# Keys loaded a second time in transposed layout, decayed by elementwise products, in place of matmul transposes

## The chip, the cores and the metric

The program runs on 1 core of one Trainium2 chip. The metric is the device time of one execution in microseconds (us), the median over several runs. The traces come from one profiled execution whose own time is given beside its span. Engines are named TensorE (PE; its weight loads PEld), VectorE (DVE), ScalarE (ACT), GpSimd (POOL) and SyncE (SP, which here only issues DMAs).

## The reference, cut to what matters

Three layers follow each other, all in fp32. Only the first is touched by the change. It is a linear recurrence over 768 steps for 4 batches x 8 heads, head dimension 48:

```
for t in range(768):
    cur    = u * k[t] outer v[t]
    y[t]   = r[t] @ (state + cur)
    state  = w[:, None] * state + k[t] outer v[t]
x = y as 3072 tokens x 384
logits = x @ phi                      # 32 slots, softmax over tokens and over slots
slot   = softmax_tokens(logits).T @ x
out_s  = relu(slot_e @ w1[e]) @ w2[e] # 8 experts, 4 slots each
x      = softmax_slots(logits) @ out_s
out    = gelu_sigmoid(x @ w_in) @ w_out   # w_in, w_out held as 64-bit floats
```

## The kernel before, in words

The recurrence is computed in chunks. A unit is one batch and one chunk of 128 steps; there are 24 units, taken two batches at a time, and each covers all 8 heads as 4 pairs. Powers of w stand in tables: `tr` holds the factor for every step of a chunk, in a layout with the head dimension on partitions (128 partitions x 4 pairs x 128 steps), and `tab` the reversed factor with steps on partitions. With r multiplied by `tr` and k by the reversed factor, a chunk is a masked product of r and k, then a product with v, plus a product of r with the carried state.

One pass of the loop over n (line 657) writes the instructions of several units into the in-order queues of the engines, in an order set by hand (`tc.manual_schedule`, line 361). For pass n they are: `r_decay(n+2)`, line 495, VectorE, r times `tr`, both in SBUF; `st_a(n+1)`, line 514, 16 matmuls of k and r into PSUM, whose halves are then masked, one by VectorE (line 518) and one by a ScalarE copy and a GpSimd select (lines 521, 522); `st_q`, line 531, matmuls on `rk`, copied to `qT` by ScalarE (line 534); `st_n(n-1)`, line 549, transposes of the output, with VectorE's add into `xn` (line 553); `bonus(n)`, line 538, a GpSimd product of v and a broadcast factor; `k_turn(n+2)`, lines 500 to 505: four TensorE transposes of the decayed key `kp` into the PSUM tile `k_ps`, a ScalarE copy of it to `kT`, and VectorE's product `rk` of r and `k_ps`; `st_y`, `st_u`, `st_v` (lines 603, 576, 614); `st_s`, VectorE's update of the carried state (lines 591, 592) and its ScalarE copies (line 595); `st_x` (lines 558, 561); `k_decay(n+3)`, line 488, a GpSimd product of k and `tab` (VectorE for the first units). Every fourth pass runs the token softmax of a group of four units ahead of the transposes of the next (lines 169 to 237).

From pass 3 on, `wload` (line 635) adds to each pass three of the four VectorE operations that decode a slice of `w_in` from 64-bit floats (lines 94 to 107). Of these all but line 94 read two tensors in SBUF. `wload` also issues DMAs of `w_in` and of the expert weights: 18 of them, 768 KB each, for experts 0 to 3 and half of expert 4, paced by the pass. All DMAs are issued by SyncE in program order; r of unit n+5 (`ld_r`, 256 KB) and k and v of unit n+5 (`ld_kv`, 384 KB) in pass n. The buffers of four of the five k and v tiles lie in the place of the second weight of expert 4 (`stage`, line 310), so the DMAs of that weight come after the last pass.

After the loop follow the slot inputs, the experts (lines 865 to 896), whose weights are partly loaded only then, and the last layer with its 1152 matmuls at line 1178.

Of the kernel before, what the change touches and what calls it, by code (L numbers as in the profile page):

```python
# [8 lines left out]
F32 = mybir.dt.float32  # L9
# [6 lines left out]
ALU = mybir.AluOpType  # L16
# [5 lines left out]
def attn_moe_mlp_kernel(  # L22
    ctx: ExitStack,
    tc: tile.TileContext,
    rT: bass.AP,
    kvn: bass.AP,
    r: bass.AP,
    w: bass.AP,
# [8 lines left out]
    nc = tc.nc  # L37
# [3 lines left out]
    E, _, FE = w1.shape  # L41
# [258 lines left out]
    with ExitStack() as actx:  # L300
# [4 lines left out]
        def at(shape, name, dt=F32, bufs=1):  # L305
            return ap.tile(shape, dt, tag=name, name=name, bufs=bufs)

        NRT, NKV, NKP, NXN, NXT, NA = 5, 5, 3, 6, 4, 2

        stage = wts.tile([P, FT * DM], F32, tag=f"wb{NSL}", name="stage")  # L310
        used = [0]

        def part(shape):

# [18 lines left out]
        qT = at([P, P], "qT")  # L333
        rt = [at([P, NP, P], f"rt{i}") for i in range(NRT)]
        kp = [at([P, H, HP], f"kp{i}") for i in range(NKP)]
        kT = at([P, NP, P], "kT")
        rk = at([P, NP, P], "rk")
        am = [at([P, 2, NP, P], f"am{i}") for i in range(NA)]
        sbd = [at([P, NP, 2, HP], f"sbd{i}") for i in range(2)]
# [11 lines left out]
        def ld_r(i):  # L351
            if 0 <= i < NU:
                b, c = units[i]
                nc.sync.dma_start(out=rt[i % NRT].rearrange("p q t -> p (q t)"), in_=rT[b, c])

        def ld_kv(i):
            if 0 <= i < NU:
                b, c = units[i]
                nc.sync.dma_start(out=kv[i % NKV], in_=kvn[b, c * P:(c + 1) * P])

        with tc.manual_schedule():
            wc = at([P, NP], "wc")
            uc = at([P, NP], "uc")
            nc.sync.dma_start(out=wc, in_=w)
            ld_kv(0)
            ld_r(0)
            nc.sync.dma_start(out=uc, in_=u)
            for i in range(1, NRT):
                ld_kv(i)
                ld_r(i)  # L370
                if i == 2:
                    nc.sync.dma_start(out=phn, in_=phi.rearrange("(k p) s -> p k s", p=P))
            make_identity(nc, ident)
# [73 lines left out]
            def small_tables():  # L447
                tt(out=w128.unsqueeze(2), in0=pb[:, :, 16:17], in1=pb[:, :, 16:17], op=ALU.mult)

                for m in range(2):  # L450
                    tt(
                        out=ubd[HP * m:HP * m + HP, :, m:m + 1], in0=uc[HP * m:HP * m + HP].unsqueeze(2),
                        in1=pa_[HP * m:HP * m + HP, :, 1:2], op=ALU.mult,
                    )
# [31 lines left out]
            def k_decay(i, eng=nc.gpsimd):  # L486
                if ok(i):
                    eng.tensor_tensor(
                        out=kp[i % NKP][:, :, 0:D], in0=kv[i % NKV][:, 0], in1=tab, op=ALU.mult
                    )  # L490

            def r_decay(i):
                if ok(i):
                    x = rt[i % NRT]
                    tt(out=x, in0=x, in1=tr, op=ALU.mult)

            def k_turn(i):

                if ok(i):
                    for q in range(NP):  # L500
                        nc.tensor.transpose(  # L501
                            k_ps[:, q, :], kp[i % NKP][:, 2 * q:2 * q + 2, :].rearrange("p h d -> p (h d)"), ident
                        )
                    nc.scalar.copy(out=kT, in_=k_ps)  # L504
                    tt(out=rk, in0=rt[i % NRT], in1=k_ps, op=ALU.mult)  # L505

            def st_a(i):

                if ok(i):
                    t = [ps.tile([P, NP, P], F32, tag="a", name="pa", bufs=2) for _ in range(2)]  # L510
                    for q in range(NP):
                        for m in range(2):
                            p = slice(HP * m, HP * m + D)
                            nc.tensor.matmul(  # L514
                                t[m][:, q, :], kT[p, q, :], rt[i % NRT][p, q, :], start=True, stop=True
                            )
                    x = am[i % NA]
                    nc.vector.copy_predicated(
                        out=x[:, 0], mask=mask.unsqueeze(1).to_broadcast([P, NP, P]), data=t[0]
                    )  # L520
                    nc.scalar.copy(out=x[:, 1], in_=t[1])  # L521
                    nc.gpsimd.affine_select(  # L522
                        out=x[:, 1], in_=x[:, 1], pattern=[[0, NP], [1, P]], compare_op=ALU.is_gt, fill=0.0,
                        base=0, channel_multiplier=-1,
                    )
# [102 lines left out]
                return [xn[:, (4 * g + m) % NXN, :] for m in range(4)]  # L628


            eq = [(e, n) for e in range(NSL + 1) for n in range(4 if e < NSL else 2)]
            wq = [(g, n) for g in range(NWI) for n in range(4)]
            NEQ = len(eq)

# [18 lines left out]
            put_tab()  # L653
            fill(9)
            small_tables()
            k_decay(0, nc.vector)
            for n in range(-2, NU + 2):
                g, m = divmod(n - 5, 4)
                first, second = (0 <= g < NG and m == x for x in range(2))
                second = second and g < NG - 1  # L660
                r_decay(n + 2)
                if second:
                    grp.rows(g, (1,))
                st_a(n + 1)
                st_q(n + 1)
                if -1 <= n <= 0:
                    fill(8)
                if first:
                    g1(g)
                st_n(n - 1)  # L670
                if second:
                    grp.sums(g, g3_x(g), n=(0,))
                bonus(n)
                k_turn(n + 2)
                if n == -2:
                    fill(8)
                if first:
                    grp.maxima(g)
                if second:
                    grp.sums(g, None, n=(1,))  # L680
                st_y(n)
                st_u(n)
                st_v(n)
                st_s(n)
                st_x(n)
                if n == -1:
                    fill(7)
                if first and g < NG - 1:
                    grp.rows(g, (0,))
                k_decay(n + 3, nc.gpsimd if n > -1 else nc.vector)  # L690
                if n == 1:
                    flag()
                    flag_out()
                    selector()
                if n == 4:
                    n_ok = nc.values_load(flg, min_val=0, max_val=P * NP)
                if n >= 0:
                    ld_r(n + NRT)
                    ld_kv(n + NKV)
                wload(n)  # L700
                if n == NU - 1:
                    while eq:
                        load_w(*eq[0], wts, eq[0][0])
                        eq.pop(0)
                    for a in (2, 3):
                        load_w(NSL, a, wts, NSL)

            slot_inputs(
# [509 lines left out]
                    dec_two(n + 4)  # L1218


_INS = ["rT", "kv", "r", "w_l", "u_l", "moe_phi", "moe_w1", "moe_w2", "moe2_w_in", "moe2_w_out"]
_OUTS = [((3072, 384), "float32")]


# [39 lines left out]
```

## Time and profile before

| | |
|---|---|
| median of 3 runs | 437.15 us (436.16 to 437.56) |
| profiled execution | 435.27 us, span 433.8 us |
| TensorE, busy | 414.3 us (96%) |
| VectorE, busy | 263.3 us (61%) |
| ScalarE, busy | 189.5 us (44%) |
| GpSimd, busy | 61.2 us (14%) |
| DMA | 59.50 MB, mean 137 GB/s |
| granted TensorE clock, mean | 0.996 |

The shares are means over stages that differ. The recurrence lasts from about 10 to 155 us; the matmuls at line 1178 fill the second half of the span, where GpSimd does nothing and VectorE's share is below its mean. To read what a change of the recurrence is worth, one looks at the stretches of the recurrence, at the length of a pass, and at what each queue does in a pass.

### The profile page before, as it was taken

The page shows a single profiled execution, that of the slowest core. Times are in us where ns is not written, and L with a number is a line of the kernel's source. Part 1 is how long each engine was busy: PE and PEld are TensorE (multiplying, and loading weights), DVE is VectorE, ACT ScalarE, POOL GpSimd, SP SyncE. Part 2 cuts the span into 40 slices and gives each one's busy share as a digit, 9 for nine tenths or more (in the row PEclk, how much of TensorE's full clock was granted, in tenths as well). Part 3 has the DMA queues.
Part 4 walks back from the last instruction along what each step waited for, and adds up shares of the span by engine and source line. Part 5 has one row for each costly group of instructions (what it writes and reads, how often), then busy time and mean ns, then how long its engine had stood idle before and what let it go on. Part 6 is the DMA issues. An engine that isn't in the chain of part 4 may idle for free.

```text
span 433.8 us, 9269 instructions
## 1 busy us (share of the span) xinstructions
PE 414.3 (96%) x3746; PEld 362.3 (84%) x3746; DVE 263.3 (61%) x491; ACT 189.5 (44%) x450; POOL 61.2 (14%) x89
## 2 busy tenths in 40 slices
PE   8999999999999989987899999999999999999996
PEld 7877777777777755444799999999999999999996
DVE  5678788878788854235699974444454444544441
ACT  2455566564665633334668764222232222422221
POOL 4343443444334210000000000000000000000000
PEclk9999999999999999998999999999999999999999
DMA  7355987798868377994333003000030000300003
GB/s 250 142 173 184 284 304 240 243 322 256 286 204 288 101 278 251 382 382 156 80 121 111 0 2 109 2 0 2 0 110 0 2 0 2 109 2 0 2 0 109
DMA packets 36003, 59.50 MB, mean 137 GB/s; under 512 B 3057, under 2 KB 21617, under 8 KB 35953
## 3 DMA queue, kind: packets, MB, share of 16 engines
q1 hardware_dynamic: 35952, 58.85, 40.4%
q8 instruction: 30, 0.49, 0.5%
q14 instruction: 21, 0.16, 0.1%
HBM read 53.53 MB, written 4.72 MB: 134 GB/s over the span
## 4 chain that ended last, share of the span: by engine, by line
PE 53%; DMA 2%; DVE 2%; ACT 1%; SPq 1%; issue 1%; ACTq 0%; DVEq 0%
PE o L1178 45%; PE hpa L1116 3%; DMA raw_a<-in_moe_w_out_dram 2%; PE hpb L1116 2%; PE sop L893 1%; PE hp L869 1%; DVE glb L1130 1%; SPq L958 1%; PE htp L881 0%; PE ga L1088 0%; ACT ggb L1119 0%; DVE w_lo L988 0%; ACT G L1100 0%; DVE ghb L1129 0%; DVE raw_a L107 0%
## 5 line engine op out<-in xcount | busy, mean ns | idle before, releaser
L1178 PE MATMUL o<-w_hi,ghb 128*128 128x384 f32 x384 | 115.9, 335 | 0.0
L1178 PE MATMUL o<-w_lo,ghb 128*128 128x384 f32 x384 | 115.7, 334 | 0.0
L1178 PE MATMUL o<-w_hi,glb 128*128 128x384 f32 x384 | 115.5, 334 | 0.0
L1119 ACT ACTIVATE ggb<-hpa 128x512 f32<-128x512 f32 x64 | 38.2, 598 | 118.0 <-PE hpa L1116 117.9
L1129 DVE CAST ghb<-ggb 128x768 fp32r<-128x768 f32 x48 | 26.9, 560 | 83.9 <-ACT ggb L1119 83.9
L1178 PEld LDWEIGHTS o<-w_hi,ghb 128*128 128x128 f32 x384 | 70.2, 188 | 2.4
L1178 PEld LDWEIGHTS o<-w_hi,glb 128*128 128x128 f32 x384 | 71.1, 188 | 0.0
L1178 PEld LDWEIGHTS o<-w_lo,ghb 128*128 128x128 f32 x384 | 71.0, 188 | 0.0
L1130 DVE TENSOR_TENSOR glb<-ggb,ghb 128x768 fp32r<-128x768 f32 x64 | 61.3, 958 | 12.7 <-ACT ghb L1127 11.1
L505 DVE TENSOR_TENSOR rk<-rt,k_ps 128x512 f32<-128x512 f32 x24 | 16.5, 688 | 21.0 <-ACT kT L504 21.0
L1116 PE MATMUL hpa<-c4T,G 96*128 96x512 f32 x64 | 25.5, 398 | 2.7 <-ACT ggb L1119 1.3
L618 ACT COPY yT<-y_ps 128x512 f32<-128x512 f32 x24 | 14.0, 585 | 31.9 <-PE y_ps L614 31.8
L514 PE MATMUL pa<-rt,kT 48*128 48x128 f32 x384 | 27.9, 285 | 0.0
L514 PEld LDWEIGHTS pa<-rt,kT 48*128 48x128 f32 x384 | 23.3, 187 | 3.8 <-issue 3.3
L522 POOL TENSOR_SCALAR_AFFINE_SELECT am<-am 128x512 f32<-128x512 f32 x24 | 15.7, 655 | 73.5 <-ACT am L521 67.8
L1119 ACT ACTIVATE ggb<-hpb 128x256 f32<-128x256 f32 x64 | 24.2, 378 | 0.0
L504 ACT COPY kT<-k_ps 128x512 f32<-128x512 f32 x24 | 14.1, 586 | 21.8 <-PE k_ps L501 21.8
L603 PE MATMUL y_ps<-rt,sbd 128*128 128x128 f32 x160 | 21.2, 276 | 0.0
L614 PE MATMUL y_ps<-am,stage 128*48 128x128 f32 x320 | 21.1, 274 | 0.0
L603 PEld LDWEIGHTS y_ps<-rt,sbd 128*128 128x128 f32 x160 | 19.4, 192 | 0.6 <-issue 0.6
L501 PE MATMUL k_ps<-ident,kp 128*128 128x128 f32 x96 | 15.1, 280 | 4.8 <-ACT qT L534 3.7
L501 PEld LDWEIGHTS k_ps<-ident,kp 128*128 128x128 f32 x96 | 10.1, 140 | 11.0 <-issue 11.0
(185 smaller groups left out, 611.3 us busy)
## 6 DMA issues: line engine op xcount, KB each, us to landing
w<-in_moe_w_dram SPq DMA_DIRECT2D x32, 768.0 KB, 7.0
stage<-in_kv_dram SPq DMA_DIRECT2D x20, 384.0 KB, 3.8
rt<-in_rT_dram SPq DMA_DIRECT2D x24, 256.0 KB, 3.8
raw<-in_moe_w_in_dram SPq DMA_DIRECT2D x16, 384.0 KB, 4.3
out_dram<-obuf SPq DMA_DIRECT2D x24, 192.0 KB, 2.0
raw_a<-in_moe_w_out_dram SPq DMA_DIRECT2D x10, 384.0 KB, 3.6
raw_b<-in_moe_w_out_dram SPq DMA_DIRECT2D x6, 384.0 KB, 6.0
kv<-in_kv_dram SPq DMA_DIRECT2D x4, 384.0 KB, 3.8
```

Of the source, the lines that this page charges most:

```text
L501: nc.tensor.transpose(k_ps[:, q, :], kp[i % NKP][:, 2 * q:2 * q + 2, :].rearrange("p h d -> p (h d)"), ident)
L504: nc.scalar.copy(out=kT, in_=k_ps)
L505: tt(out=rk, in0=rt[i % NRT], in1=k_ps, op=ALU.mult)
L514: nc.tensor.matmul(t[m][:, q, :], kT[p, q, :], rt[i % NRT][p, q, :], start=True, stop=True)
L522: nc.gpsimd.affine_select(out=x[:, 1], in_=x[:, 1], pattern=[[0, NP], [1, P]], compare_op=ALU.is_gt, fill=0.0, base=0, channel_multiplier=-1,)
L603: nc.tensor.matmul(y_ps[:, q, :], sbd[b % 2][:, q].rearrange("p m d -> p (m d)"), rt[i % NRT][:, q, :], start=(q == 0), stop=False, skip_g ...
L614: nc.tensor.matmul(y_ps[HP * m:HP * m + D, q, :], kv[i % NKV][:, 1, 2 * q + m, :], am[i % NA][:, m, q, :], start=(c == 0 and q == 0), stop ...
L1116: nc.tensor.matmul(hp, G4[:, f * P:(f + 1) * P], c4T[:, c * TB + t0:c * TB + t0 + n], start=True, stop=True)
L1119: nc.scalar.activation(out=ggb[:, i % NB_S, t0:t0 + n], in_=hp, func=AF.Gelu_apprx_sigmoid)
L1129: nc.vector.tensor_copy(out=gh, in_=gg)
L1130: nc.vector.tensor_tensor(out=gl, in0=gg, in1=gh.bitcast(F32), op=ALU.subtract)
L1178: nc.tensor.matmul(o, x, y, start=f == 0 and i == 0, stop=f == KF - 1 and i == 2)
```

## The change

The host makes a second array of k, `kT`, padded and transposed as it does for r. SyncE loads it unit by unit (`ld_kt`, 256 KB each) into six tiles that lie in the place of the first weight of expert 4. `kt_decay` multiplies such a tile in place by `tr` read backwards: units 0 to 2 on VectorE, the others on GpSimd right behind `k_decay`. `k_turn` is gone; its product `rk` stays on VectorE and reads the new tile instead of PSUM, and `st_a` reads the new tile. Since the place of expert 4's first weight is now taken, both its halves are loaded after the last pass's other DMAs, and 16 loads instead of 18 are paced by the passes. `kp` and `k_decay` stay as they are.

```diff
+        stage_k = wts.tile([P, KD * FE], F32, tag=f"wa{NSL}", name="stage_k")
+        kt = [
+            stage_k[:, i * NP * P:(i + 1) * NP * P].rearrange("p (q t) -> p q t", q=NP) for i in range(NKT)
+        ]
...
+        def ld_kt(i):
+            if 0 <= i < NU:
+                b, c = units[i]
+                nc.sync.dma_start(out=kt[i % NKT].rearrange("p q t -> p (q t)"), in_=kTd[b, c])
...
+            ld_kt(0)
+            ld_r(0)
             ld_kv(0)
-            ld_r(0)
...
             for i in range(1, NRT):
+                ld_kt(i)
+                ld_r(i)
                 ld_kv(i)
-                ld_r(i)
...
-            def k_turn(i):
-
+            def kt_decay(i, eng=nc.gpsimd):
                 if ok(i):
-                    for q in range(NP):
-                        nc.tensor.transpose(
-                            k_ps[:, q, :], kp[i % NKP][:, 2 * q:2 * q + 2, :].rearrange("p h d -> p (h d)"), ident
-                        )
-                    nc.scalar.copy(out=kT, in_=k_ps)
-                    tt(out=rk, in0=rt[i % NRT], in1=k_ps, op=ALU.mult)
+                    x = kt[i % NKT]
+                    eng.tensor_tensor(out=x, in0=x, in1=tr[:, :, ::-1], op=ALU.mult)
+
+            def r_times_k(i):
+
+                if ok(i):
+                    tt(out=rk, in0=rt[i % NRT], in1=kt[i % NKT], op=ALU.mult)
...
-                                t[m][:, q, :], kT[p, q, :], rt[i % NRT][p, q, :], start=True, stop=True
+                                t[m][:, q, :], kt[i % NKT][p, q, :], rt[i % NRT][p, q, :], start=True, stop=True
...
-            eq = [(e, n) for e in range(NSL + 1) for n in range(4 if e < NSL else 2)]
+            eq = [(e, n) for e in range(NSL) for n in range(4)]
...
+            kt_decay(0, nc.vector)
+            r_decay(0)
             k_decay(0, nc.vector)
+            kt_decay(1, nc.vector)
             for n in range(-2, NU + 2):
...
-                r_decay(n + 2)
+                if n > -2:
+                    r_decay(n + 2)
...
-                k_turn(n + 2)
+                r_times_k(n + 2)
...
                 k_decay(n + 3, nc.gpsimd if n > -1 else nc.vector)
+                if n > -2:
+                    kt_decay(n + 3, nc.gpsimd if n > -1 else nc.vector)
...
                     ld_r(n + NRT)
+                    ld_kt(n + NRT)
                     ld_kv(n + NKV)
...
-                    for a in (2, 3):
+                    for a in range(4):
                         load_w(NSL, a, wts, NSL)
```

## Rows read from the trace of the kernel before

**Rows 1.** Busy time by stretch: from:to and length, engines busy (count), clock, DMA share, GB/s
```profile
35.46:140.57 105.11, 99.78 (x1382) 79.81 (x1381) 87.40 (x162) 61.65 (x165) 41.95 (x51) 1.00 0.81 265
140.57:155.70 15.13, 14.86 (x197) 11.84 (x197) 12.21 (x25) 8.30 (x26) 3.70 (x5) 1.00 0.44 150
...
165.60:199.60 34.00, 30.70 (x372) 15.42 (x364) 13.88 (x39) 13.52 (x27) 0.31 (x1) 0.99 0.94 339
```

**Rows 2.** Timeline of TensorE around the transposes: start, length, instruction, count, idle before
```profile
110.06 0.66 PE L549 MATMUL n_ps<-ident,yT 128*128 128x128 f32 x4
111.46 0.63 PE L501 MATMUL k_ps<-ident,kp 128*128 128x128 f32 x4 [0.74 <-ACT qT L534]
111.92 1.06 PE L603 MATMUL y_ps<-rt,sbd 128*128 128x128 f32 x8
```

**Rows 3.** Groups of VectorE, 35.46 to 140.57: count | busy us, mean ns | idle
```profile
L505 DVE TENSOR_TENSOR rk<-rt,k_ps 128x512 f32<-128x512 f32 x17 | 11.7, 688 | 14.2 <-ACT kT L504 14.2
L495 DVE TENSOR_TENSOR rt<-rt,tr 128x512 f32<-128x512 f32 x17 | 11.6, 683 | 0.0
L592 DVE TENSOR_TENSOR sc<-sc,w 128x192 f32<-128x192 f32 x13 | 9.5, 729 | 0.4
...
L107 DVE SCALAR_TENSOR_TENSOR win<-sq,win 128x384 f32<-128x384 f32 x13 | 8.0, 618 | 0.3
```

**Rows 4.** Timelines of GpSimd and VectorE around 78, 66, 121 and 107 us
```profile
78.08 1.01 POOL L488 TENSOR_TENSOR kp<-stage,tab 128x384 f32<-128x384 f32 x1
...
78.33 0.69 DVE L505 TENSOR_TENSOR rk<-rt,k_ps 128x512 f32<-128x512 f32 x1 [1.20 <-ACT kT L504]
...
66.09 1.14 POOL L488 TENSOR_TENSOR kp<-stage,tab 128x384 f32<-128x384 f32 x1 [1.44 <-issue]
...
66.29 1.35 DVE L107 SCALAR_TENSOR_TENSOR win<-sq,win 128x384 f32<-128x384 f32 x1
...
121.55 0.36 DVE L592 TENSOR_TENSOR sc<-sc,w 128x192 f32<-128x192 f32 x1
...
105.61 0.83 POOL L538 TENSOR_TENSOR xn<-stage,xq 128x384 f32<-128x384 f32 x1
...
105.68 0.54 DVE L553 TENSOR_TENSOR xn<-n_ps,xn 128x384 f32<-128x384 f32 x1
...
107.37 1.00 POOL L488 TENSOR_TENSOR kp<-stage,tab 128x384 f32<-128x384 f32 x1 [0.93 <-POOL xn L538]
...
107.66 0.92 DVE L592 TENSOR_TENSOR sc<-sc,w 128x192 f32<-128x192 f32 x1
108.50 0.54 DVE L94 TENSOR_SCALAR win<-raw 128x384 int32<-128x384 int32 x1
109.08 0.56 DVE L99 SCALAR_TENSOR_TENSOR win<-raw,win 128x384 int32<-128x384 int32 x1
```

**Rows 5.** Groups of GpSimd, 35.46 to 140.57
```profile
L488 POOL TENSOR_TENSOR kp<-stage,tab 128x384 f32<-128x384 f32 x14 | 14.2, 1016 | 12.2 <-issue 8.0 <-POOL xn L538 3.2 <-DVE rk L505 1.1
L522 POOL TENSOR_SCALAR_AFFINE_SELECT am<-am 128x512 f32<-128x512 f32 x17 | 11.3, 662 | 48.7 <-ACT am L521 44.9 <-DVE xn L553 3.8
```

**Rows 6.** Timelines of VectorE and GpSimd one pass after 107 us
```profile
111.36 0.55 DVE L553 TENSOR_TENSOR xn<-n_ps,xn 128x384 f32<-128x384 f32 x1
...
111.82 0.83 POOL L538 TENSOR_TENSOR xn<-stage,xq 128x384 f32<-128x384 f32 x1
```

**Rows 7.** Timeline of the first passes
```profile
9.00 0.63 PE L501 MATMUL k_ps<-ident,kp 128*128 128x128 f32 x4 [0.27 <-DVE kp L488]
...
10.43 1.16 PE L514 MATMUL pa<-rt,kT 48*128 48x128 f32 x16
...
29.68 1.16 PE L514 MATMUL pa<-rt,kT 48*128 48x128 f32 x16
```

**Rows 8.** Timeline of SyncE's queue at the last passes, and a piece of the chain
```profile
147.67 1.02 SPq L137 DMA_DIRECT2D w<-in_moe_w_dram  x2
...
185.82 10.66 DMA raw_a<-in_moe_w_out_dram
```

More of the change, by code (lines that the diff above doesn't have):

```diff
@@ L25, in attn_moe_mlp_kernel @@
     rT: bass.AP,
+    kTd: bass.AP,
     kvn: bass.AP,
@@ L306, in at @@
             return ap.tile(shape, dt, tag=name, name=name, bufs=bufs)
-        NRT, NKV, NKP, NXN, NXT, NA = 5, 5, 3, 6, 4, 2
+        NRT, NKT, NKV, NKP, NXN, NXT, NA = 5, 6, 5, 3, 6, 4, 2
         stage = wts.tile([P, FT * DM], F32, tag=f"wb{NSL}", name="stage")
         used = [0]
+        stage_k = wts.tile([P, KD * FE], F32, tag=f"wa{NSL}", name="stage_k")
+        kt = [
+            stage_k[:, i * NP * P:(i + 1) * NP * P].rearrange("p (q t) -> p q t", q=NP) for i in range(NKT)
+        ]
         def part(shape):
@@ L335, in attn_moe_mlp_kernel @@
         kp = [at([P, H, HP], f"kp{i}") for i in range(NKP)]
-        kT = at([P, NP, P], "kT")
         rk = at([P, NP, P], "rk")
@@ L1218, in attn_moe_mlp_kernel @@
                     dec_two(n + 4)
-_INS = ["rT", "kv", "r", "w_l", "u_l", "moe_phi", "moe_w1", "moe_w2", "moe2_w_in", "moe2_w_out"]
+_INS = ["rT", "kT", "kv", "r", "w_l", "u_l", "moe_phi", "moe_w1", "moe_w2", "moe2_w_in", "moe2_w_out"]
 _OUTS = [((3072, 384), "float32")]
@@ L1237 @@
     rT[:, :, :, :D] = r.reshape(B, H // 2, 2, S // P, P, D).transpose(0, 3, 2, 5, 1, 4)
+    kT = _np.zeros_like(rT)
+    kT[:, :, :, :D] = k.reshape(B, H // 2, 2, S // P, P, D).transpose(0, 3, 2, 5, 1, 4)
     kv = _np.stack([k, v]).transpose(1, 3, 0, 2, 4)
@@ L1243 @@
     inputs = dict(
-        inputs, rT=rT.reshape(B, S // P, P, -1), kv=kv, w_l=w_l.reshape(P, -1), u_l=u_l.reshape(P, -1)
+        inputs, rT=rT.reshape(B, S // P, P, -1), kT=kT.reshape(B, S // P, P, -1), kv=kv, w_l=w_l.reshape(P, -1), u_l=u_l.reshape(P, -1)
     )
```

## The prediction

> **What bounds the kernel now.** I read the busy time by stretch first, since the share over the whole span mixes stages. The stretch from 35.46 to 140.57 us holds 17 passes of the recurrence loop, 6.18 us each (105.11 / 17), and TensorE is busy for 99.8 of its 105.1 us, VectorE for 87.4, GpSimd for 42.0; the DMA engines are busy for 0.81 of it at 265 GB/s [rows 1]. So TensorE's queue sets the pass, VectorE has 17.7 us to spare, and both GpSimd and the DMA engines have room. Behind the loop, from 165.6 to 199.6, the DMA engines work at 0.94 and the chain that ended last runs through a load [rows 1, 8]: the end follows the loop one for one only if no loads pile up there.
>
> The timeline of TensorE shows what the transposes cost in a pass. The transposes of the output start at 110.06 and take 0.66; those of the key could follow at about 110.7, start at 111.46 because they wait 0.74 us for ScalarE's copy out of the same PSUM tile, and let the next matmuls begin at 111.92 [rows 2]. That pass pays 1.2 us for them. In a pass without that wait it is 0.63 less some overlap with the next matmuls, 111.92 - 111.46 = 0.46 [rows 2].
>
> **The change part by part.** TensorE in the 17 passes: the pitch of 0.46 goes 17 times, 7.8 us, and the waits that stand directly ahead of it go with it, between nothing and 0.74 us each; I take 0.3, so 0.76 a pass and 12.9 us. TensorE would then need 105.1 - 12.9 = 92.2 us. ScalarE loses a copy per pass and bounds neither before nor after (61.7 of 105.1 us busy [rows 1]); I cost that at nothing.
>
> DMA: 24 loads of 256 KB are added, 0.262 MB each. The stretch now works 0.81 x 105.1 = 85.1 us at 265 / 0.81 = 327 GB/s, and in the loads after the loop 339 / 0.94 = 361 GB/s [rows 1]. One load costs 0.73 to 0.80 us of all engines; with up to 17 in the stretch that is 12 to 14 us, so the DMA engines need 97 to 99 us. That is room enough for the pass as it is, and a floor: no engine's gain can bring the stretch below about 97. A wait of SyncE is not added before them, because the tile that `ld_kt(n+5)` fills was last read several passes earlier.
>
> VectorE: the number of its instructions stays; `rk` reads r and the key from SBUF instead of r and PSUM. Without conflict it costs the same: 688 ns now against 683 ns for `r_decay`, which has that form [rows 3]. What changes is what it can run beside. Line 592, with two SBUF inputs, takes 0.36 us at 121.55 with GpSimd idle, and 0.92 us at 107.66, where GpSimd's product at line 488 runs from 107.37 to 108.37: it ends 0.21 us after that product does [rows 4]. Line 107 takes 1.35 us beside the product at 66.09, ending 0.41 us after it, and that product is itself lengthened, from 1.00 to 1.14 us [rows 4]. In contrast `rk`, reading PSUM, keeps its 0.69 us at 78.33 under a GpSimd product, and so do line 553, which reads PSUM, at 105.68 and line 94, with one input, at 108.50 [rows 4]. So a two-input product on GpSimd and a VectorE operation with two SBUF inputs exclude each other. The mean of line 592 is 729 ns against 0.36 us alone, and it is nearly all such waiting: 13 x 0.37 = 4.8 us [rows 3]. The Trainium skill says the same more generally (Advanced Engine Details and Errata, GPSIMD Details): GpSimd shares a read and a write interface with VectorE and conflicts with its instructions that have two SBUF inputs. The trace shows it for four lines; for `rk` from SBUF and for a select beside a two-input operation, the rule would add conflicts that no row here has.
>
> GpSimd gets one product of 512 elements a pass, `kt_decay`, which no row shows. Scaled by size from `bonus`, 0.83 for 384, it is 1.11 us; from `k_decay`, 1.00 for 384, it is 1.33 [rows 4]. I take 1.2, between them: its output is contiguous as that of `bonus`, but it reads both inputs in full as `k_decay` does. GpSimd's sum of 42.0 us becomes 42.0 + 17 x 1.2 = 62 of 105, so it isn't the bound by busy time. A page gives another price (Trainium skill, GPSIMD Engine Reference, Performance versus the Vector engine: 4497 ns for 2048 elements), which would be an estimate of 1.12 us, at the lower end; the sum below would be 1 us shorter by it. The same page's Engine selection advises against elementwise products on GpSimd, as about twice as slow as VectorE; the rows here agree (0.83 to 1.00 us for 384 elements against 0.68 for 512).
>
> Now the conflicts that are new, laid out from the pass at 105 to 110 us. First `rk`: VectorE comes to it after line 553, ending 106.22, and today waits for ScalarE's copy. Freed of that, it meets `bonus`, which ends at 106.44, a wait of 0.21; a pass later line 553 ends at 111.91 and `bonus` at 112.65, a wait of 0.74 [rows 4, 6]. Mean 0.5, so 17 x 0.5 = 8.5 us. Second, the decode of `w_in`: `kt_decay` follows right behind `k_decay`, which ends at 108.37, or behind line 592, which waits for `k_decay` and ends at 108.58. It would run until about 109.7. Line 94 may run beside it, but line 99, which today starts at 109.08, waits 0.6 us; and in three passes of four the first operation to come is itself a two-input one and waits the whole 1.1 [rows 4]. Mean (0.6 + 3 x 1.1) / 4 = 0.98, less 0.14 that a waiting operation has behind it already (line 107 ended 0.41 after the product and not the 0.56 that line 99 takes alone): 0.84, so 17 x 0.84 = 14.3 us. Line 592's waits stay as they are. VectorE then needs 87.4 + 8.5 + 14.3 = 110.2 us in the stretch where it had 105.1. Queued behind a waiting operation on VectorE are `r_decay` and the mask of line 518, and TensorE's matmuls at line 514 and ScalarE's copies of the state wait for those; the lag can't be made up, since VectorE no longer idles. So VectorE takes TensorE's place as the bound, and the stretch grows by 5.1 us.
>
> Bounds of these waits: none at all (GpSimd's products fall beside line 518, line 553 and other PSUM readers, about 0.73 + 0.55 a pass) gives VectorE 87.4 and leaves the DMA floor of 97, a gain of 8; the full 0.74, the full 1.33, and a wait of `r_decay` behind the select (0.66 us each [rows 5]) in every pass give 87.4 + 17 x 2.73 = 134, a loss of 29, which would need every operation to meet its worst neighbour.
>
> The first passes: four key turns go ahead of the pass at 29.68. The first matmuls of line 514 start at 10.43 behind the turn of 9.00 and its copy [rows 7]; the key tile can be decayed before, so 0.7 us goes there. Three further turns at 0.46 to 0.76 are 1.4 to 2.3 us. Against this stand three `kt_decay` on VectorE, 3 x 0.68 = 2.0, partly beside TensorE's fill work, and 1.3 MB more of first loads, 4 us at 327 GB/s, of which the leading keys and r come earlier than today and k and v later. I take a gain of 2.0, within 0 to 3.
>
> The two loads of expert 4 are issued at 147.67 today [rows 8]. Moved behind the last pass they still wait only for the last reader of the key tiles, one pass before the end, so they come about a microsecond later, into a stretch whose DMA share is 0.44 [rows 1]: nothing. Were that cover gone, they would cost 2 x 0.786 MB / 361 GB/s = 4.4 us in the chain of loads. The loop's last passes have no `kt_decay`, and I cost them at nothing.
>
> Sum: -2.0 + 5.1 = +3.1 us, 435.27 + 3.1 = 438.4 for an execution like the profiled one. Its time lies 1.9 us under the median of the runs shown, so the forecast is 437.15 + 3.1 = 440.2, about 440.
>
> **The rivals.** *Faster: the port is shared without loss.* GpSimd's products drift to where VectorE reads PSUM, since once VectorE lags, GpSimd runs on TensorE's phase. For it: GpSimd has slack of 40 us in the stretch, and VectorE's operations without conflict amount to 1.3 us a pass or more. Against it: `kt_decay` sits directly behind `k_decay`, and what VectorE does then is line 592 and the decode, nearly all with two SBUF inputs. With all new waits gone the stretch falls to the DMA floor, 97: -8 - 2 = -10, 427. With half of them gone (11.4 us), VectorE needs 98.8: -6.3 - 2.0, 429. It decides where the new waits stay under 17.7 us in the 17 passes, 1.04 a pass; there the stretch is level with today's.
>
> *Slower by more: the select joins.* Line 522 also uses GpSimd's port; if `r_decay` waits behind it, for 0.4 us of its 0.66 in every pass [rows 5], that is 6.8 us more: 447. For it: VectorE lags by then, so `r_decay` falls where ScalarE's copy and the select do. Against it: no row shows a VectorE operation waiting for a select. A `kt_decay` of 1.33 adds 2 more.
>
> *No change:* the new waits just eat VectorE's spare 17.7 us and the first passes' gain is small: 436 to 438.
>
> **How the numbers follow.** The forecast, 438.5 to 444, has 0.40; the faster rival, up to 435.8, 0.36; the slower one, above 444, 0.10; no change 0.14. About 0.3%, 1.3 us, is what a measurement can tell from none. Faster 0.36, same 0.14, slower 0.50. The likeliest case's own range is 438.5 to 444; the range that leaves out 2 in 10 reaches to half of the faster rival and over the slower one's 447: 428 to 450.
>
> **What would show it.** In the page after, line 501 is gone and TensorE's busy time in the loop falls by some 10 us while VectorE's rises to nearly the whole loop. Lines 99, 103, 107 and `rk` show means well above 0.56 and 0.69; a `kt_decay` of 1.1 to 1.35 us; first matmuls of line 514 near 9.7. The forecast is wrong if those means stay as they are, if VectorE still idles in the passes, or if the loop's passes come out near 5.7 us; a wait of `kt_decay` for its DMA would be a cause that I have not priced.

## The result and the profile after

The changed kernel takes 440.32 us (median of 14 runs, 437.92 to 442.68) against 436.14 us for the kernel before (14 runs, 433.46 to 437.56): a ratio of 1.0104, 95% interval 1.0081 to 1.0126. It is slower by about 1%. The profiled execution took 441.75 us, its span is 440.1 us against 433.8.

The first line of the page after gives busy time and share of the span for each engine:

```profile
PE 406.5 (92%) x3650; PEld 353.7 (80%) x3650; DVE 291.8 (66%) x494; ACT 175.2 (40%) x426; POOL 100.6 (23%) x110
```

TensorE lost 8 us of work and ScalarE 14; VectorE gained 28, GpSimd 39. VectorE got three products more, all before the passes looked at here; the rest of its gain is nearly all time spent waiting inside instructions that count as busy. Where that happens shows in the busy time by stretch, in the same 17 passes as [rows 1], from the first matmul of one pass to the same matmul 17 passes later; the second row is what follows, to a point one output step later than the end of 140.57:155.70 in [rows 1]:

```profile
35.39:145.09 109.70, 94.07 (x1313) 73.50 (x1312) 106.48 (x160) 51.81 (x148) 72.33 (x68) 1.00 0.84 285
145.09:163.50 18.41, 15.83 (x198) 12.02 (x197) 15.26 (x29) 8.77 (x26) 6.86 (x7) 1.00 0.55 171
```

The stretch is 4.6 us longer than the 105.11 of before. TensorE, which was busy for 99.8 of it, idles for 15.6 now, while VectorE is busy for all but 3.2. The groups of VectorE in this stretch (count | busy us, mean ns | idle), which answer to [rows 3], show where its time went:

```profile
L517 DVE TENSOR_TENSOR rk<-rt,stage_k 128x512 f32<-128x512 f32 x17 | 19.1, 1121 | 0.0
L507 DVE TENSOR_TENSOR rt<-rt,tr 128x512 f32<-128x512 f32 x17 | 14.6, 857 | 0.0
L530 DVE COPY_PREDICATED am<-mask,pa 128x512 f32<-128x512 int32 x17 | 12.4, 729 | 0.0
L100 DVE SCALAR_TENSOR_TENSOR win<-raw,win 128x384 int32<-128x384 int32 x13 | 11.5, 888 | 0.3
L108 DVE SCALAR_TENSOR_TENSOR win<-sq,win 128x384 f32<-128x384 f32 x12 | 11.5, 955 | 0.8
L104 DVE SCALAR_TENSOR_TENSOR win<-raw,win 128x384 int32<-128x384 int32 x13 | 9.3, 715 | 0.3
...
L604 DVE TENSOR_TENSOR sc<-sc,w 128x192 f32<-128x192 f32 x13 | 8.2, 632 | 0.4
...
L189 DVE TENSOR_TENSOR bx<-nm_run 128x1 f32<-128x1 f32 x3 | 3.6, 1189 | 0.1
L187 DVE TENSOR_TENSOR nm_run<-nm_run 128x1 f32<-128x1 f32 x3 | 1.9, 635 | 0.1
```

Four of these lines stand in the same view of before, beside [rows 3], under the numbers 99, 103, 188 and 186 instead of 100, 104, 189 and 187:

```profile
L99 DVE SCALAR_TENSOR_TENSOR win<-raw,win 128x384 int32<-128x384 int32 x13 | 7.3, 563 | 0.3
L103 DVE SCALAR_TENSOR_TENSOR win<-raw,win 128x384 int32<-128x384 int32 x13 | 7.2, 556 | 0.3
L188 DVE TENSOR_TENSOR bx<-nm_run 128x1 f32<-128x1 f32 x3 | 1.9, 622 | 0.1
L186 DVE TENSOR_TENSOR nm_run<-nm_run 128x1 f32<-128x1 f32 x3 | 0.5, 159 | 0.1
```

Every line after with two inputs in SBUF has a mean well above what it takes alone, but line 530, which reads PSUM, has kept its 0.73 us. Line 189 works on one element per partition and takes 1.19 us in the mean, against 0.16 with the product on VectorE (first experiment below); lying in wait is nearly all that it does. The groups of GpSimd, beside [rows 5]: the new product, `k_decay`, and the select. `k_decay` had a mean of 1016 ns and has 1353, the select 662 and 724, so the waiting goes both ways:

```profile
L512 POOL TENSOR_TENSOR stage_k<-stage_k,tr 128x512 f32<-128x512 f32 x17 | 23.2, 1365 | 0.0
L500 POOL TENSOR_TENSOR kp<-stage,tab 128x384 f32<-128x384 f32 x14 | 18.9, 1353 | 0.8 <-POOL xn L550 0.6
...
L534 POOL TENSOR_SCALAR_AFFINE_SELECT am<-am 128x512 f32<-128x512 f32 x17 | 12.3, 724 | 36.4 <-ACT am L533 31.5 <-PE n_ps L561 4.9
```

One pass in timelines (start, length), first GpSimd, then VectorE:

```profile
106.24 1.39 POOL L512 TENSOR_TENSOR stage_k<-stage_k,tr 128x512 f32<-128x512 f32 x1
108.48 0.65 POOL L534 TENSOR_SCALAR_AFFINE_SELECT am<-am 128x512 f32<-128x512 f32 x1 [0.85 <-ACT am L533]
109.10 1.13 POOL L550 TENSOR_TENSOR xn<-stage,xq 128x384 f32<-128x384 f32 x1
...
111.60 1.27 POOL L512 TENSOR_TENSOR stage_k<-stage_k,tr 128x512 f32<-128x512 f32 x1
```

```profile
106.42 1.62 DVE L100 SCALAR_TENSOR_TENSOR win<-raw,win 128x384 int32<-128x384 int32 x1
108.08 0.56 DVE L104 SCALAR_TENSOR_TENSOR win<-raw,win 128x384 int32<-128x384 int32 x1
108.74 0.80 DVE L108 SCALAR_TENSOR_TENSOR win<-sq,win 128x384 f32<-128x384 f32 x1
109.47 1.31 DVE L507 TENSOR_TENSOR rt<-rt,tr 128x512 f32<-128x512 f32 x1
...
111.78 1.64 DVE L517 TENSOR_TENSOR rk<-rt,stage_k 128x512 f32<-128x512 f32 x1
```

Line 100 starts 0.18 us into `kt_decay`, takes 1.62 us and ends at 108.04, 0.41 us after the product (107.63); line 104, with no product running, takes 0.56. Line 108 meets the select and ends 0.41 us after it. Line 507 meets `bonus`, 1.31 us instead of 0.68; line 517, the product `rk`, meets `kt_decay` of the next pass, 1.64 instead of 0.69; both end 0.55 us after the product that they met. Of the five shown, four are late in a single pass.

### The profile page after: what moved, and what is told of

It is laid out like the page before. It is cut to its first block, busy times and chain, and to the rows that moved or that the text cites. A ratio compares the mean times of both kernels' runs of the same rounds, so it can differ in the third digit from the quotient of the medians.

```text
span 440.1 us, 9114 instructions
## 1 busy us (share of the span) xinstructions
PE 406.5 (92%) x3650; PEld 353.7 (80%) x3650; DVE 291.8 (66%) x494; ACT 175.2 (40%) x426; POOL 100.6 (23%) x110
## 4 chain that ended last, share of the span: by engine, by line
PE 53%; DMA 2%; DVE 2%; ACT 1%; SPq 1%; issue 0%; ACTq 0%; DVEq 0%
PE o L1197 44%; PE hpa L1135 3%; DMA raw_a<-in_moe_w_out_dram 2%; PE hpb L1135 2%; PE sop L912 1%; PE hp L888 1%; SPq L977 1%; DVE glb L1149 1%; PE htp L900 0%; PE ga L1107 0%; ACT ggb L1138 0%; DVE w_lo L1007 0%; ACT G L1119 0%; DVE ghb L1148 0%; PE ctp L954 0%
## 5 line engine op out<-in xcount | busy, mean ns | idle before, releaser
L534 POOL TENSOR_SCALAR_AFFINE_SELECT am<-am 128x512 f32<-128x512 f32 x24 | 18.2, 759 | 55.9 <-ACT am L533 46.2
L512 POOL TENSOR_TENSOR stage_k<-stage_k,tr 128x512 f32<-128x512 f32 x21 | 28.5, 1358 | 0.0
L526 PE MATMUL pa<-rt,stage_k 48*128 48x128 f32 x384 | 27.9, 285 | 0.0
L526 PEld LDWEIGHTS pa<-rt,stage_k 48*128 48x128 f32 x384 | 23.3, 187 | 3.9 <-issue 3.2
L517 DVE TENSOR_TENSOR rk<-rt,stage_k 128x512 f32<-128x512 f32 x24 | 24.8, 1033 | 0.0
L500 POOL TENSOR_TENSOR kp<-stage,tab 128x384 f32<-128x384 f32 x17 | 22.7, 1334 | 1.3 <-POOL xn L550 0.9
L607 ACT COPY sbd<-sc 64x192 f32<-64x192 f32 x40 | 14.0, 350 | 17.3 <-DVE sc L604 14.0
```

The costliest lines, as they stand in the source:

```text
L500: eng.tensor_tensor(out=kp[i % NKP][:, :, 0:D], in0=kv[i % NKV][:, 0], in1=tab, op=ALU.mult)
L512: eng.tensor_tensor(out=x, in0=x, in1=tr[:, :, ::-1], op=ALU.mult)
L517: tt(out=rk, in0=rt[i % NRT], in1=kt[i % NKT], op=ALU.mult)
L526: nc.tensor.matmul(t[m][:, q, :], kt[i % NKT][p, q, :], rt[i % NRT][p, q, :], start=True, stop=True)
L534: nc.gpsimd.affine_select(out=x[:, 1], in_=x[:, 1], pattern=[[0, NP], [1, P]], compare_op=ALU.is_gt, fill=0.0, base=0, channel_multiplier=-1,)
```

## The experiments

Unless another base is named, each kernel is the changed one with the edit shown. The stretch of 17 passes is marked by the same matmuls throughout; it measured 105.1 us before and 109.7 after. The kernel before had medians of 434.65 to 437.11 us beside these runs, so differences between two kernels are taken from their ratios to it, times 435 us. By the intervals of the ratios such a difference is known to about 1.5 us either way.

**The new product on VectorE.** If GpSimd's part in the conflict is the cost, `kt_decay` is cheaper on the engine that is already full.

```diff
-                    kt_decay(n + 3, nc.gpsimd if n > -1 else nc.vector)
+                    kt_decay(n + 3, nc.vector)
```

> The changed kernel with kt_decay on VectorE for all units. Theory 1 (the shared port: a two-input product on GpSimd and a VectorE operation with two SBUF inputs exclude each other): the waits behind kt_decay go, some 14 us of the 17 passes from 35 to 145 us, and 17 x 0.6 = 10 us of work come to VectorE; about 4 us less than the changed kernel, 436 to 437; decode operations (lines 95 to 108) back at 0.56 us mean except beside k_decay. Theory 2 (VectorE is simply out of time, ports aside): 10 us more in its queue make it about 450. Theory 3 (the added loads slow the loop): no change, 440.

Measured: 432.34 us, ratio to the kernel before 0.9948 (0.9927 to 0.9969): better than any theory said, and (1.0104 - 0.9948) x 435 = 6.8 us under the change as made. The stretch, and its groups of VectorE:

```profile
34.29:136.88 102.59, 94.40 (x1314) 74.46 (x1313) 98.94 (x177) 51.49 (x148) 49.11 (x51) 0.98 0.91 306
```

```profile
L517 DVE TENSOR_TENSOR rk<-rt,stage_k 128x512 f32<-128x512 f32 x17 | 14.8, 871 | 0.0
...
L512 DVE TENSOR_TENSOR stage_k<-stage_k,tr 128x512 f32<-128x512 f32 x17 | 11.7, 688 | 0.0
...
L100 DVE SCALAR_TENSOR_TENSOR win<-raw,win 128x384 int32<-128x384 int32 x13 | 8.2, 629 | 0.3
...
L108 DVE SCALAR_TENSOR_TENSOR win<-sq,win 128x384 f32<-128x384 f32 x12 | 6.6, 554 | 0.8
```

VectorE got 11.7 us of work and is busy for 7.5 us less. The three decode lines are back near what they take alone (554 to 629 ns), and `rk` fell from 1121 to 871 ns, with `bonus` and `k_decay` still on GpSimd. This is the run that settles the cause: the waits go with the engine that the product runs on. The Trainium skill (GPSIMD Engine Reference, Engine selection) advises VectorE for elementwise products; the runs agree, with 6.8 us to gain on an engine that has no time to spare.

**The product left out.** What do its waits and its work cost together? The kernel leaves out the 21 products that GpSimd does, 17 of them in the stretch, so its keys are not decayed.

```diff
-                if n > -2:
-                    kt_decay(n + 3, nc.gpsimd if n > -1 else nc.vector)
+                if n == -1:
+                    kt_decay(n + 3, nc.vector)
```

> The changed kernel without kt_decay for units 3 to 23, so their keys are not multiplied by the decay; the loads stay. Theory 1: VectorE loses the waits behind it; the 17 passes fall from 109.7 to about 97 us, where the loads or VectorE (87 + 8.5 us of work and old waits) set the pace: 427 to 429. Theory 2: VectorE's own work is the same, so 438 to 440. Theory 3: the loads stay, so 440.

Measured: 423.62 us, 0.9737 (0.9712 to 0.9761), lower than expected.

```profile
33.55:129.12 95.57, 91.78 (x1314) 73.20 (x1313) 91.66 (x162) 51.57 (x148) 47.40 (x51) 1.00 0.96 330
```

So `kt_decay` costs (1.0104 - 0.9737) x 435 = 16.0 us of time on GpSimd and (0.9948 - 0.9737) x 435 = 9.2 on VectorE, though there 17 of its 21 executions are already 11.7 us of work in the stretch. And the rest of the change, with the transposes gone, is worth (1 - 0.9737) x 435 = 11.4 us by itself: the gain was there, and the product took back more than that, 9.2 us even on VectorE and 6.8 on top by its place on GpSimd. The DMA engines work at 0.96 in this stretch, TensorE and VectorE for 91.8 and 91.7 of its 95.6 us, so which of them sets its length isn't shown; the 97 us that I put the floor of the loads at was at least 1.4 too high.

`rk` still waits here:

```profile
L517 DVE TENSOR_TENSOR rk<-rt,stage_k 128x512 f32<-128x512 f32 x17 | 17.7, 1038 | 0.0
```

The decode lines are at 592 to 608 ns without the product, `rk` at 1038 and not at 0.69 us. With `kt_decay` gone it meets `bonus` and `k_decay`.

**`rk` from PSUM again.** `rk` reads its second input from PSUM, as before, with all else as in the change. It reads 128 elements per partition of that tile four times over, so its values are not the wanted ones.

```diff
-                    tt(out=rk, in0=rt[i % NRT], in1=kt[i % NKT], op=ALU.mult)
+                    tt(out=rk, in0=rt[i % NRT], in1=k_ps[:, 1:2, :].to_broadcast([P, NP, P]), op=ALU.mult)
```

> The changed kernel, but the product rk reads r and a region of a PSUM tile instead of r and the key tile, so that its values are not those wanted; instruction count and sizes stay. Theory 1: rk falls from a mean of 1.03 us to 0.69 and no longer holds bonus or k_decay back; 17 x 0.35 = 6 us less in the loop, 434 to 435. Theories 2 and 3: the operation has the same size, so no change, 440.

Measured: 432.48 us, 0.9939 (0.9918 to 0.996), a little lower than expected: the 1.03 us that I started from is `rk`'s mean over the whole span, in the stretch it is 1.12. The stretch, and the group of `rk`:

```profile
35.80:138.14 102.34, 92.93 (x1314) 73.39 (x1313) 99.03 (x161) 51.42 (x148) 67.36 (x68) 1.00 0.90 306
```

```profile
L517 DVE TENSOR_TENSOR rk<-rt,k_ps 128x512 f32<-128x512 f32 x17 | 11.5, 677 | 0.0
```

The instruction writes the same 512 elements on the same engine; one input's place differs. It takes 677 ns instead of 1121, 17 x 0.44 = 7.5 us, and the stretch loses 7.4. That isolates the price of `rk`'s two SBUF inputs, the first conflict of the prediction.

**The loads alone.** The kernel before, with the second keys loaded into the new tiles and not read, and expert 4's loads moved as in the change.

```diff
+            ld_kt(0)
...
+                    ld_kt(n + NRT)
...
-                    for a in (2, 3):
+                    for a in range(4):
                         load_w(NSL, a, wts, NSL)
```

> The kernel before with the change's loads alone: the transposed keys are loaded in the changed kernel's order and never read, the weights of expert 4 are loaded as in the changed kernel, and the TensorE turns stay. Theory 1: 0 to 1 us over the kernel before, 436 to 437. Theory 3 (the loads cost the time): 440.

Measured: 434.13 us, 0.9999 (0.9981 to 1.0018). No part of the 0 to 1 us that I allowed for shows. In the stretch the DMA share rises from 0.81 to 0.91 and nothing else moves; the theory that the loads cost the time is dead, and the 4.4 us that the moved loads could have cost were not paid:

```profile
34.47:139.59 105.12, 99.78 (x1381) 79.83 (x1380) 87.39 (x162) 61.62 (x165) 41.98 (x51) 1.00 0.91 304
```

**`kt_decay` earlier.** GpSimd does it at the start of its pass, behind the matmuls of `st_a`, instead of behind `k_decay`, so that it doesn't lie ahead of the decode.

```diff
+                if n > -1:
+                    kt_decay(n + 3)
...
-                if n > -2:
-                    kt_decay(n + 3, nc.gpsimd if n > -1 else nc.vector)
+                if n == -1:
+                    kt_decay(n + 3, nc.vector)
```

> The changed kernel with kt_decay between the select and bonus in GpSimd's queue instead of behind k_decay. Theory 1: it then falls beside line 530 and line 565, which read PSUM, and less beside the decode; the decode's waits of 0.84 us a pass shrink to about 0.2 while rk's wait grows from 0.35 to 0.6 or more: 17 x 0.4 = 7 us less, 433 to 437. Theory 2: the order doesn't matter, 440.

Measured: 434.73 us, 0.999 (0.9967 to 1.0014). The place alone returns 5.0 us, and the time lies in the range of Theory 1, but not for its reason: the decode's means stay at 762 to 866 ns, 31.2 us against 32.3, and `rk`'s mean, which was to grow, falls to 1034. VectorE is busy for 5.3 us less, spread over `rk` (1.5), lines 187 and 189 of the softmax (2.1) and the rest. The forecast of this run was right by luck.

```profile
32.60:137.38 104.78, 94.66 (x1314) 74.83 (x1313) 101.19 (x159) 51.85 (x148) 74.81 (x68) 0.98 0.90 299
```

**The bonus on ScalarE.** ScalarE does `bonus` by eight scaled copies of 48 elements; `kt_decay` stays on GpSimd.

```diff
-                    nc.gpsimd.tensor_tensor(
...
+                    for h in range(H):
+                        nc.scalar.activation(
+                            out=xn[:, i % NXN, h * D:(h + 1) * D], in_=kv[i % NKV][:, 1, h, :], func=AF.Copy,
+                            scale=xq[(i - 1) % NXT][:, DM + h:DM + h + 1],
+                        )
```

> The changed kernel with bonus (v times a factor per step and head) as eight ScalarE instructions a pass instead of one GpSimd product; kt_decay stays on GpSimd. Theory 1 (shared port): 0.83 us a pass of port time go, and with them rk's wait behind bonus; the 17 passes fall from 109.7 to about 102 us, 432 to 434. Theory 2 (VectorE out of time by its own work): 440. A rival to both: ScalarE's 8 x 0.18 = 1.5 us a pass delay its copies, on which the select and the output transposes wait: 440 or more.

Measured: 435.16 us, 1.0 (0.9969 to 1.0032), above the expected range, though 4.5 us under the change. The stretch, and ScalarE's group:

```profile
35.17:140.42 105.25, 96.31 (x1314) 75.41 (x1313) 99.07 (x159) 81.80 (x282) 55.83 (x51) 0.97 0.88 297
```

```profile
L551 ACT ACTIVATE xn<-stage,xq 128x48 f32<-128x48 f32 x103 | 24.7, 328 | 0.9 <-PE pp L222 0.8
```

A copy takes 328 ns where I had counted on 180, but eight in a row overlap: those that start at 105.10 us are done after 1.92 us, not 2.6, against the 1.5 expected. VectorE lost 7.4 us, about what Theory 1 forecast for the stretch, but it now idles for 6.2 us instead of 3.2. That it then waits for ScalarE's longer queue would fit, but no run here shows it. `r_decay` is at 683 ns again, what it takes alone, with the select still on GpSimd.

**Both moved.** The edits of the first experiment and of the one just shown together.

> The changed kernel with kt_decay on VectorE and bonus on ScalarE; GpSimd keeps k_decay and the select. Theory 1: VectorE needs 87.4 + 17 x 0.6 = 97.6 us in the 17 passes and the loads 97 to 98, so about 98 where kt_decay on VectorE alone left 102.6: 427 to 429. If ScalarE's added instructions are on the path: no better than 432.

Measured: 426.0 us, 0.978 (0.9753 to 0.9808), a little under the expected range. This version beats both kernels.

```profile
32.60:131.44 98.84, 92.76 (x1314) 73.38 (x1313) 95.76 (x176) 82.28 (x284) 30.29 (x34) 1.00 0.94 318
```

VectorE is still the bound with 95.8 of 98.8 us, but it does 11.9 us of `kt_decay` and its decode lines are at 556 to 574 ns.

**The bonus moved in the kernel before.** Does that move gain by itself, or only by the port that it frees?

> The kernel before with bonus on ScalarE and nothing else. If both moves gained because they took port time from a loop that VectorE bounds, the same move gains nothing here, where TensorE bounds the loop and the key turns stay: 435 to 438 (ScalarE then works some 92 of the 105 us of the 17 passes, and its copies may come late). If bonus on GpSimd was a cost of its own, it gains the 3 to 6 us that it gained in the changed kernels: 429 to 432.

Measured: 442.44 us, 1.0128 (1.0089 to 1.0167): slower, where I expected no change or a gain.

```profile
37.77:147.21 109.44, 100.84 (x1382) 79.89 (x1381) 80.22 (x163) 91.13 (x301) 29.26 (x34) 1.00 0.79 255
```

```profile
L505 DVE TENSOR_TENSOR rk<-rt,k_ps 128x512 f32<-128x512 f32 x17 | 11.7, 687 | 27.3 <-ACT kT L504 27.3
```

VectorE had time for its waits here and has more now (80.2 busy of 109.4), so removing them gains nothing, and the longer ScalarE queue makes its copies late: VectorE's wait for that of the transposed key grew from the 14.2 us of [rows 3] to 27.3. TensorE, which sets the pass, waits for ScalarE's copy of `qT` ahead of its transposes of the key for 5.8 us in the stretch instead of 3.6, and for `ls` ahead of line 204 for 1.8. That is over half of the 4.3 us that the stretch grew; the rest isn't traced. The same edit is worth (0.9948 - 0.978) x 435 = 7.3 us with the product on VectorE and costs 0.0128 x 435 = 5.6 us here.

**The clamp at the start.** In the profiled execution after, the first operation on the decays at line 425, a maximum and a minimum with one tensor input on 4 elements per partition, took 2.65 us against 0.48 before. Beside it lie GpSimd's memsets:

```profile
2.70 2.65 DVE L425 TENSOR_SCALAR pa<-wc 128x4 f32<-128x4 f32 x1 [0.80 <-DMA wc<-in_w_l_dram]
```

```profile
2.20 0.95 POOL L402 MEMSET am<- 128x1024 f32 x1
...
4.30 0.99 POOL L408 MEMSET sbd<- 128x512 f32 x2
```

I replaced it by two operations with two tensor inputs.

```diff
-            nc.vector.tensor_scalar(
...
+            tt(out=pa_[:, :, 1:2], in0=wc.unsqueeze(2), in1=wlim[:, 0].unsqueeze(2), op=ALU.max)
+            tt(out=pa_[:, :, 1:2], in0=pa_[:, :, 1:2], in1=wlim[:, 1].unsqueeze(2), op=ALU.min)
```

> The changed kernel, but the clamp of w at the start (one VectorE tensor_scalar on 128x4, one SBUF input) is made by two tensor_tensor operations. If the 2.4 to 2.7 us that this clamp took in three profiles of the changed family, and 0.4 to 0.5 in the others, is a wait for GpSimd's run of memsets, the two operations take 0.2 us each in every execution, the first matmuls of line 526 come at 9.3 to 10 us, the median falls by 1 to 2 us to 438.5 to 439.5 and the spread of the runs narrows. If it is a late landing of w, the start stays as it is: 440.3.

Measured: 439.76 us, 1.0089 (1.0057 to 1.012), not told apart from the change itself.

```profile
2.77 0.17 DVE L428 TENSOR_TENSOR pa<-wc,wlim 128x4 f32<-128x4 f32 x1 [0.84 <-DMA wc<-in_w_l_dram]
```

```profile
32.52:144.12 111.60, 96.80 (x1313) 75.44 (x1312) 106.46 (x160) 51.88 (x148) 72.39 (x68) 0.97 0.84 281
95.00:96.00 1.00, 0.08 (x1) 0.00 (x0) 0.93 (x3) 0.15 (x1) 1.00 (x2) 1.00 0.65 195
99.00:105.00 6.00, 5.53 (x44) 3.72 (x44) 3.67 (x7) 1.40 (x5) 1.97 (x3) 0.50 0.68 218
```

The wait at the start is gone and the 17 passes begin 2.9 us earlier (32.52 against 35.39), but they last 111.60 us, 1.9 more, with VectorE just as busy as after (106.46). What differs is TensorE: it stood nearly still from 95 to 96 (busy 0.08), and from 99 to 105 its granted clock was 0.50, the 1.2 GHz of its two levels. In the profile after, the 17 passes have a mean of 1.00. So it seems that most of what the start gained in this execution went on a spell at the lower clock behind a wait; that the spell cost the 1.9 us isn't shown by a run without it. The timed runs don't tell whether the clamp's wait was worth anything to the median.

**All three edits together.**

> kt_decay on VectorE, bonus on ScalarE and the clamp by two tensor_tensor operations. Where the loop isn't bound by VectorE alone, a start without the clamp's wait shows in the end: 425 to 426, and no execution 2 us slower than the others; where VectorE lags anyway, as with the clamp alone, no difference to both moves without it, 426.

Measured: 426.18 us, 0.9756 (0.9731 to 0.978); with the clamp and without it (426.0), no difference that these runs show.

## Why the prediction was right, and where only its sum was

The forecast was 440.0 and the measurement 440.3; the change against the kernel before is +4.2 us by the medians, where +3.1 was the sum. That 440.0 and 440.3 lie so close is luck: the kernel before measured 436.14 beside the change and not the 437.15 that I had added to. The mechanism held. The terms did not all hold, and some errors cancelled.

**TensorE's gain.** Its busy time in the 17 passes fell by 5.7 us (99.8 to 94.1), less than "some 10"; but in the run without `kt_decay`, where it waits least, it fell by 8.0, to 91.8, close to the 7.8 of the pitch and to the 92.2 that I said it would need.

**VectorE takes its place as the bound: right.** 110.2 us predicted for the stretch, 109.70 measured, but VectorE is busy for 106.5 of that and idles for 3.2, where I had it busy throughout. Setting the groups of VectorE against those of before, line by line (the lines of before are in [rows 3] and beside the groups after), the growth is: `rk` +7.4 us (predicted 8.5); the three two-input decode lines +4.2, +2.1 and +3.5, together 9.8 with one instruction fewer in the window (predicted 14.3); `r_decay` +3.0 (predicted nothing); lines 187 and 189 of the group softmax +3.1 (not seen at all); line 604 -1.3 (predicted no change). The sum, 22.0, stands beside the 22.8 predicted, but a seventh of it comes from the softmax's one-element operations, and a seventh from `r_decay`. Neighbouring operations overlap in the groups, so busy time grew by less than their sum: 19.1 us (87.4 to 106.5). And `rk`'s waits are not `bonus` alone, as I had it. Put down to the GpSimd instruction that ended last within each execution, they are 3.8 us of `kt_decay` of the next pass and 2.6 of `bonus`.

**`kt_decay` at 1.2 us.** Its shortest execution is 1.256 us and its mean 1.365. The bounds of 1.11 to 1.33 hold for the shortest; a mean includes its own waits behind VectorE, which I had not put into that price. The 1.11 scaled from `bonus` and the 1.12 set beside it lie below the shortest.

**The conflict itself.** The rows before showed it for lines 592 and 107, two lines and not the four that I named. The rows after show it for `rk`, for `r_decay` and for the select, of which no row before spoke. The Trainium skill (SBUF — State Buffer, SBUF: two separate sides) calls the pair of ports that both engines share an exclusive lock, held for a whole instruction by the one that starts first; the timelines agree (line 100 ends 0.41 us after `kt_decay`, line 108 0.41 us after the select).

**The first passes: wrong.** I took a gain of 2.0 us and the profile shows 0.1 (the 17 passes begin at 35.39 against 35.46). The first matmul of `st_a` came at 12.30 and not near 9.7, because of the 2.65 us at line 425 and, behind it, TensorE's lower clock (0.71 in the mean from 10 to 13.5 us). The long wait is no part of the change: the kernel before with only `bonus` moved has it too, 2.69 us, and three variants of the changed kernel (the product on VectorE, both moved, the product earlier) have 0.41 to 0.48; there `st_a` begins at 8.6 to 9.7, and the 17 passes begin 1.2 to 2.9 us before the 35.46 of before. With the clamp alone replaced, the nearest comparison, they begin at 32.52, 2.9 us earlier. So with an undisturbed start the term had the right size, within the 0 to 3 that I allowed, and in this execution it was lost. But the starts scatter: without `kt_decay` the passes begin at 33.55 despite a clamp of 2.50 us, and with the loads alone at 34.47.

**The last passes: wrong.** I costed them at nothing, because they have no `kt_decay`. But the first of them still has one, the last of the 21: it runs from 146.46 for 1.38 us, and line 108 beside it takes three times its 0.55. VectorE also came into this pass late, with a queue full of held-up work:

```profile
146.64 1.61 DVE L108 SCALAR_TENSOR_TENSOR win<-sq,win 128x384 f32<-128x384 f32 x1
```

TensorE in this pass:

```profile
145.09 1.16 PE L526 MATMUL pa<-rt,stage_k 48*128 48x128 f32 x16
...
148.01 0.85 PE L176 MATMUL lp<-xq,phn 128*32 128x128 f32 x18 [1.19 <-ACT xq L576]
...
152.93 0.33 PE L205 MATMUL ltp<-ident,et 128*128 128x128 f32 x1 [0.53 <-ACT ls L193]
...
153.29 1.16 PE L526 MATMUL pa<-rt,stage_k 48*128 48x128 f32 x16
```

The same pass before starts at 140.57 and ends with this row:

```profile
147.18 1.16 PE L514 MATMUL pa<-rt,kT 48*128 48x128 f32 x16
```

With a group softmax in it, the pass takes 8.20 us where it took 6.61; TensorE waits for ScalarE, which waits for VectorE (2.04 us for line 604, 2.79 for line 187). From the end of the 17 passes to the first matmul of the last layer it is 69.07 us instead of 67.00.

**The moved loads: right.** Nothing piled up behind the loop: the load in the chain there started 6.4 us later than in [rows 8] and took as long as before:

```profile
192.18 10.73 DMA raw_a<-in_moe_w_out_dram
```

In the profiled executions the parts are then -0.1 + 4.6 + 2.1 - 0.3 (the last layer) = +6.3, the whole difference of the spans; the prediction had -2.0 + 5.1 + 0. The medians differ by 4.2, and the runs of the change spread over 4.8 us. The profiled execution after lies 1.4 us above its median and that of before 0.9 below; a start without the 2.65 us and a varying clock would give such a spread, but the timed runs have no traces, so that stays argued.

**The rivals.** The faster one, products that drift to where VectorE reads PSUM, is refuted by the means of the decode. The slower one, the select, was half right: its mechanism exists, as line 108 shows, but `r_decay`'s whole growth is 3.0 us and not 6.8, and most of that is `bonus`. By the GpSimd instruction that ended last within it, 2.5 us are `bonus` and 0.4 the select, and with `bonus` on ScalarE `r_decay` is back at 683 ns.

## What to carry to other kernels

Before a product goes to GpSimd to relieve a full VectorE, ask what VectorE does in the same microseconds: where it reads two tensors from SBUF, the two exclude each other in these traces, and here the product cost 16 us of time on the "free" engine and 9 on the full one. Removing work from the bound engine (11.4 us here) pays only if its replacement isn't put where it stops the next engine in line; a PSUM operand (`rk` at 677 ns instead of 1121) or ScalarE (`bonus` there) were ways round it here. But the move of `bonus` was worth 7 us where VectorE bounded the loop and cost 6 where TensorE did.

## What the runs showed of the hardware that I had not expected

- A VectorE operation with one SBUF input can wait too: line 425 took 0.41 to 0.48 us in five profiles (that of before, where it ends at 3.18 behind GpSimd's first large memset, among them) and 2.17 to 2.69 in five others (after it ends at 5.35, behind the memsets shown), while two two-input operations in its place took 0.17 each beside the same memsets. The Trainium skill (SBUF — State Buffer, SBUF: two separate sides) has the distinction: an operation in a mode that uses both ports contends with any GpSimd operation, one with two SBUF inputs only with those that read SBUF. The 0.17 us beside memsets, which read nothing, agree; that line 425 runs in such a mode no run here shows. Why it gets in behind one memset in some executions and behind several in others is open.
- The one-input operation at line 95, on int32, is hardly held up: 570 ns in the mean against 543 before.
- ScalarE's scaled copy of 48 elements per partition with a scale per partition takes 328 ns; eight in a row are done in 1.92 us, for what GpSimd does in 0.83 [rows 4].
- A wait of TensorE can have a second price. After the near standstill at 95 us, the clock was 0.50 for 6 us and TensorE's busy time in the stretch rose by 2.7 us (94.1 to 96.8). In the kernel with the product earlier the clock was 0.50 from 67 to 69, after a microsecond (65 to 66) without any matmul. In these two runs, where VectorE bounds the loop, TensorE's waits were long enough for such a spell to follow.
